# Dealing the MLP's hidden columns over the partitions in turn: longer runs for w2, a column step in w1's weights, alpha loaded in place

## The chip, the cores and the metric

The kernel runs on one core of one Trainium2 chip. A core has a matrix engine (TensorE, in the profile PE, with its weight loads listed apart as PEld), three engines that work on tiles (VectorE, DVE; ScalarE, ACT; GpSimd, POOL), a queue processor (SyncE, SP), and 16 DMA engines that move data between the chip's memory and the core's own memory of 128 partitions (SBUF). TensorE writes into a second memory, PSUM, here six free banks of 512 columns and a separate pair of banks called A_ps.

The metric is the device time of one execution, in microseconds; lower is better. A comparison of two kernels uses executions of both on the same chip.

## The reference

A linear attention with a decay per head, followed by an MLP. For each batch and head, with blocks of 64 positions:

```python
intra = (q k^T * Dmask) v            # Dmask[i, j] = lam ** (i - j) for i >= j, else 0
inter = (q * lam ** (pos + 1)) @ kv_state
out   = intra + inter
kv_state = lam ** 64 * kv_state + (k * lam ** (63 - pos))^T v
```

q, k and v are 4 batches x 8 heads x 768 positions x 64, float32. The result, as 3072 tokens x 512 columns (x), goes into

```python
h = x @ w_in                         # w_in 512 x 2048
s = sin(alpha * h)                   # one alpha per column of h
g = h + s * s / (alpha + 1e-9)
y = g @ w_out                        # w_out 2048 x 512, y 3072 x 512
```

A hidden column f belongs to column f of w_in, alpha[f], and row f of w_out. In which order the 2048 hidden columns are worked on does not change y.

## The kernel before, in words

**Tiling.** The tokens are worked on in 6 chunks of 512 (index c). The attention of a chunk consists of four quads (t), each for some heads and positions of some batches: scale q and k with powers of lam (tags qs, ks), cast v (vs), transpose (Tq, Tk on TensorE for the first eight quads, a DMA transpose DT for the rest), the score matmuls S into A_ps, the mask (tag mask, line 914 for the first eight quads, 1092 later), the output matmuls O and the state Z, and the copy of the result into xT (tags x; line 988 in the first eight quads), which is the MLP's input, already transposed. A_ps has one copy, so the scores of a quad wait for the mask of the quad before.

The hidden columns are cut into 16 groups of 128 (index m). For a chunk and a group, grp_A (lines 1205 to 1249) does h^T = w1^T x with four matmuls: the stationary operand is 128 columns of w1 (128 x 128), the moving one is xT (512 tokens wide, or 256 where a group is done in halves: three pairs of groups in each of the chunks 0 and 1). So a partition of the result holds a hidden column. ACT then takes the sine with alpha as a scale per partition (tag sin, line 1231), one of POOL, DVE and ACT squares it (sq), and DVE forms g with r = 1 / (alpha + 1e-9) as a factor per partition (tag g, line 1243) into gT. grp_B (line 1283) multiplies gT with the 16 tiles of w2 (128 hidden columns x 512) for 128 tokens at a time and accumulates in PSUM; ACT or DVE copies the result out and a DMA stores it.

**Weights and alpha.** w1 is 128 partitions x 4 x 2048 and w2 is 128 x 16 x 512, both bfloat16, converted by POOL's DMAs on the way from float32. w_block (line 678) issues nine of them: w1 in a first block of two halves (w0, w0b) and three of 512 columns (w1, w2, w3), and w2 in four blocks of 512 rows (tags w4 to w7). Group m stands in columns 128 m to 128 m + 127 of w1, and row 128 m + p of w_out goes to partition p of tile m, in runs of one row (2 KB). alpha_ops (line 759) loads alpha as 16 rows of 128, transposes it on TensorE with the small identity identf (POOL, line 753), copies it out on ACT (tag alpha, line 765), adds 1e-9 on POOL (line 767) and takes the reciprocal on DVE (line 769).

**What sets the order.** Every operation is recorded with its engine, what it reads and writes, and an assumed duration (rec, rec_pe). The list ORDER in TUNE, written out by tag, fixes the order on each engine's queue; an engine does its list strictly in turn, so that a waiting operation holds up those behind it. schedule (line 287) runs through these lists with the assumed durations. It picks the PSUM banks, and before 60 us of its own time it puts matmuls on zeros (fill, line 641) where it expects TensorE to idle; their number comes from its assumed times. emit (line 478) turns what each operation depends on into semaphore waits. Operations without a name get tags c0, c1, ... in the order in which they are recorded.

**Where alpha's steps stand.** On ACT the issue of alpha's load comes after cT2.1. On POOL aeps (c30) stands between the issues of the weight blocks w3 and w2, with w4 next. On DVE the reciprocal (c31) stands between ks3.1 and Z0.1, mask2 and x1, the last of which writes a part of xT for the first MLP matmuls (A0.4h0e on TensorE). On TensorE the transpose (alpha T) stands between S1 and I0.

Of the kernel before, what the change touches and what calls it, by code (L numbers as in the profile page):

```python
# [5 lines left out]
ALU = mybir.AluOpType  # L6
# [71 lines left out]
    ORDER={'ACT': ['lam', 'c0', 'quad k0.1', 'c11', 'c13', 'c14', 'cT2.1', 'alpha in', 'c17', 'vs1', 'cT1.0', 'Zi0.1',  # L78
# [468 lines left out]
def bass_lightning_attn__then__act_snake_kernel(  # L547
# [36 lines left out]
    with es:  # L584
# [43 lines left out]
        alpha_r = sb("alpha_r", [NM, 128], F32)  # L628
        identf = sb("identf", [NM, NM], F32)
# [47 lines left out]

        def w_block(j, after=(), soft=()):
            if j == 0:
                for y in range(2):  # L680
                    cs = slice(256 * y, 256 * y + 256)
                    rec("POOL", lambda e, cs=cs: e.dma_start(
                        w1[:, :, cs], moe_w_in[:, cs].rearrange("(c p) f -> p c f", p=128)), 0, 0.8,
                        writes=[f"w1.0.{y}"], slot=f"w1_0{y}", work=1.6, weight=42.0, after=after, soft=soft,
                        tag="w0b" if y else "w0")
            elif j < 4:
                cs = slice(512 * j, 512 * (j + 1))
                src = moe_w_in[:, cs].rearrange("(c p) f -> p c f", p=128)
                wblk[j] = rec("POOL", lambda e: e.dma_start(w1[:, :, cs], src), writes=[f"w1.{j}"],
                              slot=f"w1_{j}", work=3.0, weight=80.0, after=after, soft=soft, tag=f"w{j}")  # L690
            else:
                j2 = j - 4
                src = moe_w_out[512 * j2:512 * (j2 + 1), :].rearrange("(m p) d -> p m d", p=128)
                wblk[j] = rec("POOL", lambda e: e.dma_start(w2[:, 4 * j2:4 * (j2 + 1), :], src),
                              writes=[f"w2.{j2}"], slot=f"w2_{j2}", work=3.0, weight=80.0, after=after, soft=soft,
                              tag=f"w{j}")

        def consts():
# [52 lines left out]
            for i in range(RZ):  # L751
                rec("DVE", lambda e, i=i: e.memset(Zi[i][:, :, :], 0.0), 0.2, writes=[f"Zi.{i}.0", f"Zi.{i}.1"])
            rec("POOL", lambda e: e.affine_select(
                out=identf[:, :], in_=maskf[0:NM, 0:NM], pattern=[[-1, NM]], compare_op=ALU.not_equal, fill=1.0,
                base=0, channel_multiplier=1), 0.2, reads=["maskf"], writes=["identf"])
# [3 lines left out]
        def alpha_ops():  # L759
            rec("ACT", lambda e: e.dma_start(alpha_r[:, :], moe_alpha.rearrange("(m p) -> m p", p=128)),  # L760
                writes=["alpha_r"], slot="alpha", work=0.1, weight=9.0, desc=16, tag="alpha in")
            vb = P.bank()
            rec_pe(lambda e: e.transpose(m_ps[vb.i][:, 0:NM], alpha_r[:, :], identf[0:NM, 0:NM]), [(FULL, 0.1)],
                   ["alpha_r", "identf"], [vb.key], claim=vb, tag="alpha T")
            rec("ACT", lambda e: e.copy(alpha_sb[:, :], m_ps[vb.i][:, 0:NM]), 0.2, reads=[vb.key], writes=["alpha"],
                frees=[vb], tag="alpha")
            rec("POOL", lambda e: e.tensor_scalar_add(aeps_sb[:, :], alpha_sb[:, :], 1e-9), 0.26,
                reads=["alpha"], writes=["aeps"])
            rec("DVE", lambda e: e.reciprocal(r_sb[:, :], aeps_sb[:, :]), 0.25, reads=["aeps"], writes=["r"])
# [435 lines left out]
        def grp_A(c, m, sq="POOL", half=None, early=0):  # L1205
# [10 lines left out]
            def pe(e, kcs=range(NKC)):  # L1216
                for i, mm in enumerate(ms):
                    for kc in kcs:
                        last = e.matmul(m_ps[vb.i][:, N * i:N * i + N], w1[:, kc, 128 * mm:128 * (mm + 1)],  # L1219
                                        xT[x][:, kc, ts], start=(kc == 0 and i == 0), stop=(kc == NKC - 1),  # L1220
                                        skip_group_check=True)
                return last
# [7 lines left out]
            for i, mm in enumerate(ms):  # L1230
                rec("ACT", lambda e, i=i, mm=mm: e.activation(  # L1231
                    t16[tt][:, N * i:N * i + N], m_ps[vb.i][:, N * i:N * i + N], ACTF.Sin,
                    scale=alpha_sb[:, mm:mm + 1]), 0.26 + N / 1200, 0.145 + N / 1200,
                    reads=[vb.key, "alpha"], writes=[f"t.{tt}"], tag=f"sin{c}.{mm}" + ("" if half is None else f"h{half}"))
# [220 lines left out]
```

## Time and profile before

| | |
|---|---|
| median of 3 executions | 213.55 us (213.46 to 213.74) |
| span of the profiled execution, first to last instruction | 211.8 us |
| the profiled execution's own time beside its span | not recorded; the median is 1.75 us above the span |
| TensorE (PE) busy | 202.6 us, 2108 matmuls listed |
| weight loads (PEld) busy | 108.9 us |
| DVE, ACT, POOL busy | 128.5, 128.7, 120.7 us |
| DMA | 33.92 MB in 86491 packets |
| granted TensorE clock, mean | 0.998 |

How to read it. A row of an instruction list gives its start from the beginning of the span and its duration in us, the engine, the line in the kernel, what it writes and reads, and in brackets how long its engine was idle before it and what ended that idle time. Rows with "x4" stand for four instructions in a row. "SPq", "ACTq" and "POOLq" are the issues of DMAs. A row of a DMA queue has its packets, the MB moved, and the time its packets took as a share of all 16 DMA engines; shares of queues add up to more than 100% where packets overlap. q0 is POOL's queue (the weights), q1 SP's (q, k, v and the transposes), q10 ACT's (lam, one k load, alpha, the results). A row of a DMA issue has how many such DMAs there were, their size by the destination's elements, and the median time from the issue to the landing. In the chain that ended last each piece is followed back to what released it.

### The profile page before, as it was taken

Reading aid. Unit: us, or ns where it says so; the run is one execution under the profiler, and the core shown is the slowest. Engines: PE = TensorE matmul, PEld = TensorE weight load, DVE = VectorE, ACT = ScalarE, POOL = GpSimd, SP = SyncE. Lnnn points to the kernel's source line nnn. Section 1 sums busy time; section 2 is a strip of 40 time slices with the busy share of each in tenths; the row PEclk is TensorE's granted clock in tenths of the full one; section 3 lists DMA queues with packets and bytes.
Section 4 is the critical chain, followed back from the end, with each engine's and each line's share of the span. In section 5 each row is a group of like instructions: output and inputs, shape, how many; then the busy total and the mean of one; then the engine's idle time right before and its main releaser. Section 6 shows DMA issues by size and latency. Waiting matters only on the chain.

```text
span 211.8 us, 5201 instructions
## 1 busy us (share of the span) xinstructions
PE 202.6 (96%) x2108; PEld 108.9 (51%) x2139; DVE 128.5 (61%) x229; ACT 128.7 (61%) x246; POOL 120.7 (57%) x135
## 2 busy tenths in 40 slices
PE   7798999999999999999999999999999999999994
PEld 5455756555774555444554455454544544444454
DVE  4598899678889971285753475474556521456700
ACT  3146899835599755767648756757786434646231
POOL 3772174511537772899945899687397335144500
PEclk9999999999999999999999999999999999999999
DMA  6999999998999968899779999957033011101214
GB/s 182 314 238 235 208 251 237 216 223 169 244 182 197 190 117 190 200 199 197 189 154 209 198 183 240 177 137 171 3 99 148 4 50 50 53 0 50 101 54 149
DMA packets 86491, 33.92 MB, mean 160 GB/s; under 512 B 68274, under 2 KB 83522, under 8 KB 86466
## 3 DMA queue, kind: packets, MB, share of 16 engines
q1 hardware_dynamic: 77552, 22.88, 55.3%
q0 software_dynamic: 4752, 4.19, 12.1%
q10 hardware_dynamic: 4162, 6.50, 8.7%
q8 instruction: 17, 0.28, 0.6%
q14 instruction: 8, 0.07, 0.1%
HBM read 27.27 MB, written 6.29 MB: 158 GB/s over the span
## 4 chain that ended last, share of the span: by engine, by line
PE 85%; DVE 6%; DMA 2%; issue 2%; ACTq 1%; SPq 1%; ACT 1%; POOL 0%; POOLq 0%
PE M_ps L1219 39%; PE M_ps L1296 36%; DMA q<-in_q_dram 2%; PE M_ps L1120 2%; PE M_ps L1100 1%; DVE gT L1243 1%; PE A_ps L1080 1%; PE M_ps L866 1%; PE M_ps L971 1%; DVE S_m L1092 1%; DVE S_m L914 1%; PE M_ps L956 1%; PE M_ps L1264 1%; DVE q2o L825 1%; PE A_ps L909 1%
## 5 line engine op out<-in xcount | busy, mean ns | idle before, releaser
L1239 POOL TENSOR_TENSOR u<-t 128x512 bf16<-128x512 bf16 x69 | 70.6, 1041 | 55.0 <-ACT t L1231 51.7
L1243 DVE SCALAR_TENSOR_TENSOR gT<-u,r_sb,M_ps 128x512 bf16<-128x512 bf16 (+1 forms) x108 | 70.2, 684 | 45.1 <-POOL u L1239 43.8
L1219 PE MATMUL M_ps<-xT,w 128*128 128x512 bf16 (+1 forms) x425 | 88.1, 355 | 0.6 <-DVE gT L1243 0.2
L1296 PE MATMUL M_ps<-w,gT 128*128 128x512 bf16 x347 | 83.6, 379 | 2.5 <-issue 1.9
L1231 ACT ACTIVATE t<-M_ps,alpha_sb 128x512 bf16<-128x512 f32 (+1 forms) x108 | 65.7, 640 | 27.7 <-PE M_ps L1219 26.0
L1219 PEld LDWEIGHTS M_ps<-xT,w 128*128 128x128 bf16 x432 | 41.4, 98 | 40.1 <-DVE gT L1243 0.5
L1296 PEld LDWEIGHTS M_ps<-w,gT 128*128 128x128 bf16 x368 | 34.3, 98 | 39.2 <-DVE gT L1243 0.4
L1044 POOL TENSOR_TENSOR qk<-k,Lk 128x512 bf16<-128x512 f32 x16 | 16.6, 1044 | 9.9 <-DMA k<-in_k_dram 9.9
L1092 DVE TENSOR_TENSOR S_m<-A_ps,maskl 128x768 bf16<-128x768 f32 x16 | 15.3, 955 | 8.5 <-PE A_ps L1080 8.4
L1312 ACT COPY osb<-M_ps 128x512 f32<-128x512 f32 x20 | 11.7, 585 | 13.4 <-PE M_ps L1296 13.4
L1044 POOL TENSOR_TENSOR qk<-q,Lq 128x512 bf16<-128x512 f32 x16 | 16.6, 1041 | 2.2 <-DMA q<-in_q_dram 2.2
L1172 ACT CAST xT<-M_ps 128x512 bf16<-128x512 f32 x16 | 9.4, 586 | 13.3 <-PE A_ps L1080 11.4
L641 PE MATMUL M_ps<-zeros 128*128 128x512 bf16 (+1 forms) x45 | 10.7, 390 | 1.4 <-DVE zeros L702 1.2
L1195 ACT CAST Zq<-Zf 64x256 bf16<-64x256 f32 x24 | 9.6, 400 | 1.4 <-DVE Zf L1185 0.7
L914 DVE TENSOR_TENSOR S_m<-A_ps,maskq 128x1024 bf16<-128x1024 f32 x8 | 9.7, 1212 | 1.0 <-PE A_ps L909 0.5
L1239 DVE TENSOR_TENSOR u<-t 128x512 bf16<-128x512 bf16 x13 | 7.3, 560 | 4.4 <-ACT t L1231 4.4
L1055 ACT CAST v<-v 128x512 bf16<-128x512 f32 x16 | 9.7, 618 | 0.3 <-DMA v<-in_v_dram 0.2
L838 POOL TENSOR_TENSOR qk<-k,Lk 128x256 bf16<-128x256 f32 (+1 forms) x7 | 4.9, 703 | 8.6 <-DMA k<-in_k_dram 8.0
L1238 ACT ACTIVATE u<-t 128x512 bf16<-128x512 bf16 x14 | 8.7, 636 | 0.3
L869 ACT COPY qkT<-M_ps 128x512 bf16<-128x512 bf16 x5 | 2.9, 587 | 7.3 <-PE M_ps L866 7.3
L641 PEld LDWEIGHTS M_ps<-zeros 128*128 128x128 bf16 x48 | 4.6, 122 | 4.4 <-issue 1.7
L1189 DVE TENSOR_TENSOR Zf<-M_ps,Zf 128x256 f32<-128x256 f32 x10 | 4.2, 418 | 4.2 <-ACT xT L1172 4.2
(87 smaller groups left out, 139.8 us busy)
## 6 DMA issues: line engine op xcount, KB each, us to landing
out_dram<-osb ACTq DMA_DIRECT2D x23, 256.0 KB, 2.8
q<-in_q_dram SPq DMA_DIRECT2D x20, 256.0 KB, 4.8
k<-in_k_dram SPq DMA_DIRECT2D x34, 128.0 KB, 4.2
v<-in_v_dram SPq DMA_DIRECT2D x32, 128.0 KB, 4.0
v<-in_v_dram SPq DMA_DIRECT2D x8, 256.0 KB, 8.2
w<-in_moe_w_out_dram POOLq DMA_DIRECT2D x4, 512.0 KB, 11.5
k<-in_k_dram SPq DMA_DIRECT2D x6, 256.0 KB, 10.5
w<-in_moe_w_in_dram POOLq DMA_DIRECT2D x3, 512.0 KB, 11.0
```

Of the source, the lines that this page charges most:

```text
L641: last = e.matmul(m_ps[i][:, 0:c], zeros[:, 0:128], zeros[:, 0:c])
L914: rec("DVE", lambda e: e.tensor_tensor(S_m[jm][:, :, :].rearrange("p (h a b) c -> p h a (b c)", h=2, a=2), Av().rearrange("p h (a x) -> p ...
L1044: rec(en, lambda e, L=L, gs=slice(g0, g0 + m): e.tensor_tensor(o[:, :, gs], i[:, :, gs], L, ALU.mult), *(((0.65, 0.58) if en == "DVE" else ...
L1055: rec("ACT", lambda e: e.copy(o, i), 0.613, 0.51, reads=rd, writes=[f"v2.{c}"], tag=f"vs{t}")
L1092: rec("DVE", lambda e: e.tensor_tensor(S_m[jm][:, :, :].rearrange("p (a b) c -> p a (b c)", a=4)[:, :, 0:192], A_ps[:, :, :].rearrange("p ...
L1195: rec(en, lambda e, rows=rows, en=en: (e.copy if en == "ACT" else e.tensor_copy)(Zq[jj][rows, :, rows], Zf[jj][rows, :, :].rearrange("p i ...
L1219: last = e.matmul(m_ps[vb.i][:, N * i:N * i + N], w1[:, kc, 128 * mm:128 * (mm + 1)], xT[x][:, kc, ts], start=(kc == 0 and i == 0), stop=( ...
L1231: rec("ACT", lambda e, i=i, mm=mm: e.activation(t16[tt][:, N * i:N * i + N], m_ps[vb.i][:, N * i:N * i + N], ACTF.Sin, scale=alpha_sb[:, m ...
L1239: return e.tensor_tensor(u16[tt][:, :], t16[tt][:, :], t16[tt][:, :], ALU.mult)
L1243: rec("DVE", lambda e, i=i, mm=mm: e.scalar_tensor_tensor(out=gT[g][:, mm, ts], in0=u16[tt][:, N * i:N * i + N], scalar=r_sb[:, mm:mm + 1] ...
L1296: last = e.matmul(m_ps[vb.i], gT[g][:, m, 128 * s4:128 * (s4 + 1)], w2[:, m, :], start=(m == 0 or (split and m == 8)), stop=(m == NM - 1 o ...
L1312: rec("ACT", lambda e: e.copy(osb[o][:, :], m_ps[vb.i]), 0.585, 0.48, reads=[vb.key], writes=[f"o.{o}"], frees=[vb], tag=f"o{gsi}")
```

## The change

The hidden columns are given to the partitions in another order. In the first 512 columns two groups share 256 neighbouring columns: partition p takes columns 2 p and 2 p + 1, one for each group. In the other 1536, four groups share 512 columns, and partition p takes four neighbours.

- w2: the rows that a partition needs are neighbours in w_out now, so a load moves runs of 2 rows (4 KB) in the first block and 4 rows (8 KB) in the others, instead of single rows of 2 KB. Bytes and number of loads stay.
- w1 is loaded as before. grp_A takes the 128 columns of a group from it with a step of 2 or 4 columns (cols).
- alpha comes straight into its place, partition by group, with two DMAs of runs of 2 and of 4 floats on ACT's queue. The identity identf, the transpose on TensorE with its PSUM bank, and the copy on ACT go away. aeps waits for both DMAs, and so does the first sine.
- ORDER has the new tags in the old places; c28 (identf) and the alpha entries are gone, c30 and c31 are now called aeps and r, and ACT's c29 is c28.

```diff
@@ ORDER
-    ... 'cT2.1', 'alpha in', 'c17', 'vs1', 'cT1.0', 'Zi0.1', 'alpha', 'x0', ... 'Zi2.0', 'c29',
+    ... 'cT2.1', 'alpha in0', 'alpha in', 'c17', 'vs1', 'cT1.0', 'Zi0.1', 'x0', ... 'Zi2.0', 'c28',
-    (DVE) ... 'mask1', 'ks3.1', 'c31', 'Z0.1', 'mask2', 'x1',
+    (DVE) ... 'mask1', 'ks3.1', 'r', 'Z0.1', 'mask2', 'x1',
-    (PE) ... 'Z1', 'Z0', 'S1', 'alpha T', 'I0',
+    (PE) ... 'Z1', 'Z0', 'S1', 'I0',
-    (POOL) ... 'w0b', 'w0', 'c28', 'ks3.0', 'vs0', 'w3', 'c30', 'w2', 'w4',
+    (POOL) ... 'w0b', 'w0', 'ks3.0', 'vs0', 'w3', 'aeps', 'w2', 'w4',
@@ w_block
+        def cols(m):
+            n, f = (2, 256 * (m // 2)) if m < 4 else (4, 512 * (m // 4))
+            return slice(f + m % n, f + 128 * n, n)
...
-                src = moe_w_out[512 * j2:512 * (j2 + 1), :].rearrange("(m p) d -> p m d", p=128)
-                wblk[j] = rec("POOL", lambda e: e.dma_start(w2[:, 4 * j2:4 * (j2 + 1), :], src),
+                n = 4 if j2 else 2
+                src = moe_w_out[512 * j2:512 * (j2 + 1), :].rearrange("(a p m) d -> p a (m d)", p=128, m=n)
+                dst = w2[:, 4 * j2:4 * (j2 + 1), :].rearrange("p (a m) d -> p a (m d)", m=n)
+                wblk[j] = rec("POOL", lambda e: e.dma_start(dst, src),
@@ consts
-            rec("POOL", lambda e: e.affine_select(
-                out=identf[:, :], in_=maskf[0:NM, 0:NM], ...), 0.2, reads=["maskf"], writes=["identf"])
@@ alpha_ops
-            rec("ACT", lambda e: e.dma_start(alpha_r[:, :], moe_alpha.rearrange("(m p) -> m p", p=128)),
-                writes=["alpha_r"], slot="alpha", work=0.1, weight=9.0, desc=16, tag="alpha in")
-            vb = P.bank()
-            rec_pe(lambda e: e.transpose(m_ps[vb.i][:, 0:NM], alpha_r[:, :], identf[0:NM, 0:NM]), [(FULL, 0.1)],
-                   ["alpha_r", "identf"], [vb.key], claim=vb, tag="alpha T")
-            rec("ACT", lambda e: e.copy(alpha_sb[:, :], m_ps[vb.i][:, 0:NM]), 0.2, reads=[vb.key], writes=["alpha"],
-                frees=[vb], tag="alpha")
+            for y, (m0, n, na) in enumerate(((0, 2, 2), (4, 4, 3))):
+                rec("ACT", lambda e, m0=m0, n=n, na=na: e.dma_start(
+                    alpha_sb[:, m0:m0 + n * na].rearrange("p (a m) -> p a m", m=n),
+                    moe_alpha[128 * m0:128 * (m0 + n * na)].rearrange("(a p m) -> p a m", p=128, m=n)),
+                    writes=[f"alpha.{y}"], slot=f"alpha{y}", work=0.2, weight=9.0, desc=128 * na,
+                    tag="alpha in" + ("" if y else "0"))
+            al = ["alpha.0", "alpha.1"]
             rec("POOL", lambda e: e.tensor_scalar_add(aeps_sb[:, :], alpha_sb[:, :], 1e-9), 0.26,
-                reads=["alpha"], writes=["aeps"])
-            rec("DVE", lambda e: e.reciprocal(r_sb[:, :], aeps_sb[:, :]), 0.25, reads=["aeps"], writes=["r"])
+                reads=al, writes=["aeps"], tag="aeps")
+            rec("DVE", lambda e: e.reciprocal(r_sb[:, :], aeps_sb[:, :]), 0.25, reads=["aeps"], writes=["r"], tag="r")
@@ grp_A
-                        last = e.matmul(m_ps[vb.i][:, N * i:N * i + N], w1[:, kc, 128 * mm:128 * (mm + 1)],
+                        last = e.matmul(m_ps[vb.i][:, N * i:N * i + N], w1[:, kc, cols(mm)],
...
-                    reads=[vb.key, "alpha"], writes=[f"t.{tt}"], ...
+                    reads=[vb.key, "alpha.0", "alpha.1"], writes=[f"t.{tt}"], ...
```

More of the change, by code (lines that the diff above doesn't have):

```diff
@@ L77 @@
     FSL=0.05,
-    ORDER={'ACT': ['lam', 'c0', 'quad k0.1', 'c11', 'c13', 'c14', 'cT2.1', 'alpha in', 'c17', 'vs1', 'cT1.0', 'Zi0.1',
[1 row of a table removed]
+    ORDER={'ACT': ['lam', 'c0', 'quad k0.1', 'c11', 'c13', 'c14', 'cT2.1', 'alpha in0', 'alpha in', 'c17', 'vs1', 'cT1.0', 'Zi0.1',
[1 row of a table added]
                    'sin0.4h0', 'x3', 'sin0.2h0', 'sin0.5h0', 'sin0.7', 'sin0.3h0', 'sin0.1', 'sin0.4h1', 'sq0.1',
@@ L627, in bass_lightning_attn__then__act_snake_kernel @@
         Lk = sb("Lk", [128, NE, H], F32)
-        alpha_r = sb("alpha_r", [NM, 128], F32)
-        identf = sb("identf", [NM, NM], F32)
         alpha_sb = sb("alpha_sb", [128, NM], F32)
@@ L752, in consts @@
                 rec("DVE", lambda e, i=i: e.memset(Zi[i][:, :, :], 0.0), 0.2, writes=[f"Zi.{i}.0", f"Zi.{i}.1"])
-            rec("POOL", lambda e: e.affine_select(
-                out=identf[:, :], in_=maskf[0:NM, 0:NM], pattern=[[-1, NM]], compare_op=ALU.not_equal, fill=1.0,
-                base=0, channel_multiplier=1), 0.2, reads=["maskf"], writes=["identf"])
             rec("ACT", lambda e: e.activation(junk[:, :], maskf[:, 0:1], ACTF.Sin), 1.3,
@@ L1233, in grp_A @@
                     scale=alpha_sb[:, mm:mm + 1]), 0.26 + N / 1200, 0.145 + N / 1200,
-                    reads=[vb.key, "alpha"], writes=[f"t.{tt}"], tag=f"sin{c}.{mm}" + ("" if half is None else f"h{half}"))
+                    reads=[vb.key, "alpha.0", "alpha.1"], writes=[f"t.{tt}"], tag=f"sin{c}.{mm}" + ("" if half is None else f"h{half}"))
             def square(e):
```

10 rows, old and new, of the table ORDER are left out of this document.

## The prediction

> **What bounds the kernel now.** I read the page first: its busy shares, then the chain that ended last.
>
> ```profile
> span 211.8 us, 5201 instructions
> PE 202.6 (96%) x2108; PEld 108.9 (51%) x2139; DVE 128.5 (61%) x229; ACT 128.7 (61%) x246; POOL 120.7 (57%) x135
> PE 85%; DVE 6%; DMA 2%; issue 2%; ACTq 1%; SPq 1%; ACT 1%; POOL 0%; POOLq 0%
> ```
>
> TensorE looks full and carries 85% of the chain, but its busy time also counts matmuls on zeros, and a share is a mean over stages. So next the busy time by stage (columns: stretch, its length, then busy us and instructions of PE, PEld, DVE, ACT, POOL, the granted clock, the DMA share, GB/s).
>
> ```profile
> 24.00:60.00 36.00, 35.41 (x402) 21.47 (x406) 30.66 (x64) 26.30 (x57) 14.63 (x17) 1.00 1.11 220
> 60.00:110.00 50.00, 48.94 (x544) 24.98 (x552) 34.34 (x57) 36.11 (x68) 38.34 (x38) 1.00 0.93 184
> 110.00:160.00 50.00, 48.84 (x559) 25.07 (x566) 25.93 (x39) 33.27 (x60) 37.81 (x38) 1.00 0.82 157
> 160.00:205.50 45.50, 45.13 (x258) 21.10 (x261) 20.25 (x30) 21.27 (x35) 19.00 (x19) 1.00 0.13 47
> ```
>
> From 24 to 205.5 us TensorE idles 0.59 + 1.06 + 1.16 + 0.37 = 3.2 us of 181.5, at full clock. A transfer that ends sooner has almost nothing to win there. What can move the end is the start of that dense stretch, and the length of its matmuls. So I followed the chain, and the instructions around it, before 24 us.
>
> ```profile
> 16.53 0.97 PE M_ps L641 x4
> 18.58 0.70 DVE xT L988
> ```
> ```profile
> 9.11 0.34 ACTq L760 DMA_DIRECT2D alpha_r<-in_moe_alpha_dram  x1
> 11.84 0.39 POOL L753 TENSOR_SCALAR_AFFINE_SELECT identf<-maskf 16x16 f32<-16x16 f32 x1
> 14.91 0.17 ACT L765 COPY alpha_sb<-M_ps 128x16 f32<-128x16 f32 x1 [0.56 <-PE M_ps L763]
> 15.18 0.26 POOL L767 TENSOR_SCALAR aeps_sb<-alpha_sb 128x16 f32<-128x16 f32 x1 [0.92 <-ACT alpha_sb L765]
> 15.50 0.81 POOL L689 DMA_DIRECT2D w<-in_moe_w_in_dram  x1
> 15.97 0.42 DVE L838 TENSOR_TENSOR qk<-k,Lk 128x256 bf16<-128x256 f32 x1
> 16.30 0.25 DVE L769 RECIPROCAL r_sb<-aeps_sb 128x16 f32<-128x16 f32 x1
> 16.32 0.75 POOL L694 DMA_DIRECT2D w<-in_moe_w_out_dram  x1
> 16.47 0.23 DVE L999 COPY Zf<-M_ps 128x128 f32<-128x128 f32 x1
> 16.61 1.21 DVE L914 TENSOR_TENSOR S_m<-A_ps,maskq 128x1024 bf16<-128x1024 f32 x1
> 18.58 0.69 DVE L988 CAST xT<-M_ps 128x512 bf16<-128x512 f32 x1 [0.76 <-PE M_ps L926]
> 25.67 1.04 POOL L1239 TENSOR_TENSOR u<-t 128x512 bf16<-128x512 bf16 x1 [8.60 <-ACT t L1231]
> ```
>
> The instruction to watch is the reciprocal of alpha (L769, tag r). It sits in DVE's fixed order, with no idle time around it, in front of Zf, the mask of quad 2 and the write of xT (L988) that the first MLP matmuls read. The only slack behind it is the 0.76 us that DVE waits before L988.
>
> **The change, part by part.**
>
> *Alpha's removed steps.* Out go POOL's identf (0.39 us), a TensorE transpose of 16 rows, and ACT's copy (0.17 us, after 0.56 idle). TensorE fills the same stretch with zeros, ACT and POOL are waiting there, and DVE, which sets the pace, loses nothing: 0. The second alpha transfer costs ACT one more issue of 0.34 us; if ACT were not waiting there it would cost that, and it is the cost without cover. POOL's aeps and DVE's r stay, in place.
>
> *Alpha's transfer.* Before: 16 runs of 512 B, one per DMA engine. After: runs of 8 B (2 floats, 256 of them) and of 16 B (4 floats, 384): 640 runs, so 40 per engine plus 2 semaphore writes, 42 packets. They share the engines with the weights (queue q0) and with the loads of q, k, v (q1). Rows, in this order: the transfer of alpha; q10, alpha's queue, in 13.0 to 13.5; q0 and q1 in 13 to 14; q1 in 14 to 15, 15 to 16 and 16 to 17.
>
> ```profile
> alpha_r<-in_moe_alpha_dram ACTq DMA_DIRECT2D x1, 8.0 KB, 4.9
> ...
> q10 hardware_dynamic: 29, 0.01, 6.9%
> ...
> q0 software_dynamic: 135, 0.14, 81.0%
> q1 hardware_dynamic: 139, 0.07, 34.8%
> ...
> q1 hardware_dynamic: 289, 0.15, 59.3%
> ...
> q1 hardware_dynamic: 189, 0.15, 58.5%
> ...
> q1 hardware_dynamic: 164, 0.16, 59.1%
> ```
>
> In 13 to 14 the two queues move 135 and 139 packets although one's are far larger: the engines take one packet from each queue in turn. So a queue that always has a packet gets about 139 / 16 = 8.7 turns per us on an engine, then 18, 11.8 and 10.3 in the next three. Alpha's packets ran from about 13.1 (29 of its 32 lie before 13.5) and it landed at 9.11 + 4.9 = 14.0. From 13.1, 42 turns are 7.8 + 18 + 11.8 = 37.6 by 16.0, and 4.4 / 10.3 = 0.4 more: 16.4, and 0.4 from last packet to landing as before: 16.8. Its own turns, and a second transfer that starts after the first, add some tenths: I take 17.2. Ends: 14.0 (as now, if small runs share a turn) and 19.6 (all 42 at 8.7 per us, and the second transfer 1.3 us later).
>
> [...]
>
> *What waits for it.* aeps on POOL starts 0.1 us after alpha, takes 0.26, r starts 0.1 later; from r's start to the mask's start is 0.31 and the mask takes 1.21. So the mask ends at landing + 1.98, and L988 slips once that passes 18.58: a landing after 16.6. At 17.2 the slip is **0.6 us**. Behind the waiting r stand Zf, the mask, L988, then the Zq copies that quads 1 and 2 wait for; the dense stretch begins that much later, and with 3.2 us of idle spread thin over it I give nothing back. POOL waits at aeps too, and behind it L689 and L694 issue the next two weight blocks 2 us later: hidden, because those blocks queue behind an earlier one that lands at 13.45 + 11.0 = 24.5 (the weights' row of that issue is quoted below), and POOL's next work starts at 25.67. Without that cover it would be 2 us.
>
> *The w2 loads.* First the weight block issued at 13.45; then q0 in 19 to 20 (1 KB read per packet), q0 and q1 in 36 to 37 (2 KB read), q1 alone in 9 to 10, the k load issued at 27.22, and the POOL work on k.
>
> ```profile
> w<-in_moe_w_in_dram POOLq DMA_DIRECT2D x1, 512.0 KB, 11.0
> ...
> q0 software_dynamic: 212, 0.11, 78.2%
> ...
> q0 software_dynamic: 145, 0.14, 84.6%
> q1 hardware_dynamic: 145, 0.07, 36.3%
> ...
> q1 hardware_dynamic: 587, 0.29, 120.3%
> ...
> k<-in_k_dram SPq DMA_DIRECT2D x1, 256.0 KB, 11.5
> ```
> ```profile
> 39.68 0.80 POOL L838 TENSOR_TENSOR qk<-k,Lk 128x256 bf16<-128x256 f32 x1
> 45.49 0.62 POOL L838 TENSOR_TENSOR qk<-k,Lk 128x256 bf16<-128x256 f32 x1 [5.02 <-DMA k<-in_k_dram]
> ```
>
> A packet costs 0.782 x 16000 / 212 = 59 ns for 1 KB and 0.846 x 16000 / 145 = 93 ns for 2 KB, so about 25 + 34 per KB: 161 ns at 4 KB, 297 at 8 KB. Before: 2048 x 93 = 191 engine-us; after: 256 x 161 + 384 x 297 = 155. That frees 36 / 16 = 2.2 us of all engines. But turns go one for one, so beside 8 KB packets q1 gets fewer: a pair now takes 16 / 145 = 110 ns where 93 + 40 were counted (0.83), then 0.83 x 337 = 280 ns. Three blocks take 3 x 128 / 57 per us = 6.7 us instead of 10.6, in which q1 moves 384 packets instead of 971; at 587 per us alone it has caught up by 8.7. At worst a k load is 4.0 us late: the one landing at 27.22 + 11.5 = 38.7 comes by 42.7. POOL then waits at 39.68, with 5.02 idle before 45.49 to take it; the load that ends this idle comes earlier. I take 0 for the end; the ends are the 2.2 us gained, of which TensorE's idle could use perhaps 1, and 3 lost if TensorE waits for one of those loads.
>
> *The weights with a column step.* 336 matmuls of 512 columns and 96 of 256 now load weights 2 or 4 elements apart. No load in this trace steps. The rows: all loads of L1219, the nearest slower one (f32, 128 columns), the 256-column matmuls, and a run of 512-column ones.
>
> ```profile
> L1219 PEld LDWEIGHTS M_ps<-xT,w 128*128 128x128 bf16 x432 | 41.4, 98 | 40.1 <-DVE gT L1243 0.5 <-ACT xT L1172 0.4 <-issue 0.3
> ```
> ```profile
> 3.10 0.28 PEld L722 LDWEIGHTS A_ps<-lnlam,ones 1*128 1x128 f32 x1 [0.20 <-issue]
> 19.73 0.83 PE L1219 MATMUL M_ps<-xT,w 128*128 128x256 bf16 x6
> ```
> ```profile
> 159.16 3.45 PE M_ps L1219 x16
> ```
>
> The matmuls follow each other every 3.45 / 16 = 0.216 us at 512 columns and about 0.11 at 256 (0.83 for six). A load that stays near 98 ns is hidden under either: 0. At the f32 load's 280 ns it would cost 336 x 0.064 + 96 x 0.17 = 38 us. I take 0, since tile and type are those of the first row.
>
> [...]
>
> **Sum.** 0.6 us on the span. What lies around the span, 213.55 - 211.8 = 1.75 us, I leave as it is; no time of the profiled execution beside its span is given, so the sum stands on the median: **214.1 us**, slower by 0.3%. About 0.2% (0.43 us) is what a measurement can tell.
>
> **The rivals.**
> 1. *Alpha still lands before 16.6* (runs of one transfer share a turn, or the start is earlier). Then nothing on the path moves: 213.5. Against it: one-for-one counts.
> 2. *Faster.* The four zero matmuls in the chain at 16.53 (0.97 us) end just before the work that releases L988, and DVE idles 0.76 there, mask already done. The planner sets their number from its own times, from which the transpose, its bank and the copy now vanish; if it puts in one or none, and alpha lands before 15.9, L988 starts when the mask ends: up to 0.74 less, 212.8. For it: chain and idle agree; against it: the work beside them is unchanged.
> 3. *Stepped loads are slow.* From 110 ns on they show under 256 columns, from 216 under all. At twice 98: 96 x 0.086 = 8 us, 222; at the f32 price 251.
> 4. *w2's large packets starve q1*, and TensorE, whose order is fixed, waits for k: 2 to 3 us, 216.3. It decides once a k or v load for quads 5 to 7 is later than DVE and POOL can hide.
>
> **How the numbers follow.** Forecast 0.46 (its own range 213.6 to 216.5, by landings to 19.6), rivals 0.18, 0.20, 0.10, 0.06. The range 212.8 to 217.0 takes in all but rival 3 and the far ends of 2 and 4, about 0.17. Slower by over 0.2%: 0.41 of the forecast, rivals 3 and 4, 0.57; within: 0.05 and rival 1, 0.23; faster: 0.20.
>
> **What would show it.** Alpha's second transfer landing at 17 rather than 14, aeps near 17.3, r near 17.7 with an idle wait before it, L988 near 19.2, and the same spacing from there on. Weight loads of L1219 at 98 ns and the 0.216 and 0.11 us spacing would show that the step is free; w2's packets fewer (640 for 2048) and its last block landing some us sooner with TensorE no denser, that the long runs are hidden. Wrong it would be made by an alpha at 14, by loads above 110 ns, or by a wait of TensorE for k between 35 and 55 us.

## The result: 216.26 us after 213.65, and where the time went

The changed kernel took 216.26 us (median of 4 executions, 215.46 to 216.59), the kernel before 213.65 beside it (4 executions): 1.0113 times as long, 95% interval 1.0089 to 1.0136. The profiled execution took 216.31 us, 1.8 us of it outside its span.

The page of the changed kernel: the span, the busy shares and the chain that ended last.

```profile
span 214.5 us, 5193 instructions
PE 203.5 (95%) x2105; PEld 113.9 (53%) x2136; DVE 128.0 (60%) x229; ACT 128.5 (60%) x245; POOL 119.4 (56%) x134
PE 86%; DMA 7%; DVE 2%; issue 2%; ACTq 1%; SPq 1%; ACT 1%; POOL 0%; POOLq 0%
```

The busy shares say almost nothing. The chain does: DMA has gone from 2% to 7% of it. The chain's pieces in order of time name the transfer, and the instruction list before 23 us shows who waits for it.

```profile
9.15 9.63 DMA alpha_sb<-in_moe_alpha_dram
```
```profile
18.94 0.26 POOL L768 TENSOR_SCALAR aeps_sb<-alpha_sb 128x16 f32<-128x16 f32 x1 [5.10 <-DMA alpha_sb<-in_moe_alpha_dram]
19.24 0.25 DVE L770 RECIPROCAL r_sb<-aeps_sb 128x16 f32<-128x16 f32 x1 [3.27 <-POOL aeps_sb L768]
20.00 1.91 PE L639 MATMUL M_ps<-zeros 128*128 128x512 bf16 x4 [2.73 <-DVE Zf L1000]
20.68 0.68 DVE L989 CAST xT<-M_ps 128x512 bf16<-128x512 f32 x1
22.62 1.12 PE L1220 MATMUL M_ps<-xT,w 128*128 128x256 bf16 x6
```

Alpha's second transfer, issued at 9.15, lands at 18.78 us. POOL waits 5.10 us for it, DVE 3.27 us at r, and TensorE 2.73 us for the Zf that stands behind r. The write of xT (L989, L988 before) starts at 20.68, which was 18.58. Two sines, one at the start and one near the end (before, then after), show that nothing else happened later.

```profile
23.82 0.47 ACT L1231 ACTIVATE t<-M_ps,alpha_sb 128x256 bf16<-128x256 f32 x1 [0.39 <-PE M_ps L1219]
193.50 0.69 ACT L1231 ACTIVATE t<-M_ps,alpha_sb 128x512 bf16<-128x512 f32 x1 [0.24 <-PE M_ps L1219]
```
```profile
26.46 0.47 ACT L1232 ACTIVATE t<-M_ps,alpha_sb 128x256 bf16<-128x256 f32 x1 [0.39 <-PE M_ps L1220]
196.22 0.69 ACT L1232 ACTIVATE t<-M_ps,alpha_sb 128x512 bf16<-128x512 f32 x1 [0.23 <-PE M_ps L1220]
```

The lag is 26.46 - 23.82 = 2.64 us at the second sine and 196.22 - 193.50 = 2.72 at this late one. The whole loss is there by 26 us, and 170 us of dense work carry it unchanged to the end. But xT was only 20.68 - 18.58 = 2.10 us late. The other half microsecond appears between 20 and 24 us, where the busy times by stage show the granted clock (the column behind POOL's).

```profile
20.00:21.00 1.00, 1.00 (x3) 0.44 (x3) 1.00 (x2) 0.98 (x3) 0.87 (x2) 0.50 1.25 220
21.00:22.00 1.00, 1.00 (x11) 0.16 (x12) 0.89 (x4) 0.25 (x1) 0.00 (x0) 0.50 1.22 215
22.00:23.00 1.00, 1.00 (x26) 0.74 (x25) 0.70 (x3) 0.80 (x4) 0.00 (x0) 0.50 1.24 208
23.00:24.00 1.00, 1.00 (x13) 0.90 (x11) 0.99 (x1) 1.00 (x1) 0.00 (x0) 0.88 1.24 204
```

After its wait TensorE runs at half clock. With 0.91 in the stretch from 19 to 20 us and 0.88 from 23 to 24 it lasts 0.18 + 3 + 0.24 = 3.4 us. The six 256-column matmuls at 22.62 take 1.12 us instead of 0.83.

Why alpha is late shows in the queues, packets by window of 1 us: 13 to 14 and 14 to 15 of the changed kernel, then 14 to 15 of the kernel before.

```profile
q0 software_dynamic: 136, 0.14, 81.6%
q1 hardware_dynamic: 134, 0.07, 33.5%
q10 hardware_dynamic: 133, 0.00, 7.5%
...
q0 software_dynamic: 156, 0.12, 72.9%
q1 hardware_dynamic: 163, 0.08, 39.5%
q10 hardware_dynamic: 158, 0.00, 8.9%
```
```profile
q0 software_dynamic: 128, 0.10, 59.8%
q1 hardware_dynamic: 289, 0.15, 59.3%
```

136, 134 and 133: the three queues get the same number of packets, although the share of the engines' time is 81.6% for one and 7.5% for the other. A packet of alpha is one run of 8 or 16 bytes (with two more on each engine, 672 in all, as the prediction counted). In the profiled execution of the kernel before, the weights' queue had a lull from 14 to 15 us, and q1 got 289 packets; in the changed kernel's all three queues stayed full, and there were 163. The lull was that execution's, not the kernel's: POOL's weight issues stood some 0.4 us later in it (7.59 us for the first, 7.18 in the changed kernel), ahead of everything that the change touches on POOL. In the other 13 traces of this case the first weight issue stands at 7.09 to 7.28 us, so the lags above are taken against a start that was some 0.4 us late.

The other two parts of the change, in the groups of loads, the queues' totals, and the queues at 38 to 39 us of the changed kernel:

```profile
L1220 PEld LDWEIGHTS M_ps<-xT,w 128*128 128x128 bf16 x432 | 46.2, 109 | 36.1 <-ACT xT L1173 0.4 <-DVE gT L1244 0.4 <-issue 0.3
```
```profile
q0 software_dynamic: 3344, 4.19, 11.1%
...
w<-in_moe_w_out_dram POOLq DMA_DIRECT2D x4, 512.0 KB, 8.7
...
q0 software_dynamic: 48, 0.19, 92.8%
q1 hardware_dynamic: 54, 0.03, 14.5%
```

The loads of w1 take 109 ns on the mean (98 before; the mean mixes two steps, see the run with a step of 8), under matmuls that follow each other every 216 ns where they are 512 columns wide. w2's packets of 8 KB take 0.928 x 16000 / 48 = 309 ns each, and its loads land in 8.7 us (11.5 before).

### The profile page after: what moved, and what is told of

It reads as the page before. It is cut to its first block, busy times and chain, and to the rows that moved or that the text cites. A ratio compares the mean times of both kernels' runs of the same rounds, so it can differ in the third digit from the quotient of the medians.

```text
span 214.5 us, 5193 instructions
## 1 busy us (share of the span) xinstructions
PE 203.5 (95%) x2105; PEld 113.9 (53%) x2136; DVE 128.0 (60%) x229; ACT 128.5 (60%) x245; POOL 119.4 (56%) x134
## 4 chain that ended last, share of the span: by engine, by line
PE 86%; DMA 7%; DVE 2%; issue 2%; ACTq 1%; SPq 1%; ACT 1%; POOL 0%; POOLq 0%
PE M_ps L1220 39%; PE M_ps L1297 36%; DMA alpha_sb<-in_moe_alpha_dram 4%; PE M_ps L1121 2%; DMA q<-in_q_dram 2%; PE M_ps L1101 1%; PE A_ps L1081 1%; PE M_ps L867 1%; PE M_ps L972 1%; PE M_ps L639 1%; PE M_ps L1265 1%; PE M_ps L957 1%; PE A_ps L910 1%; ACTq L1276 1%; PE M_ps L1132 1%
## 5 line engine op out<-in xcount | busy, mean ns | idle before, releaser
L1220 PEld LDWEIGHTS M_ps<-xT,w 128*128 128x128 bf16 x432 | 46.2, 109 | 36.1 <-ACT xT L1173 0.4
L1093 DVE TENSOR_TENSOR S_m<-A_ps,maskl 128x768 bf16<-128x768 f32 x16 | 15.3, 955 | 8.6 <-PE A_ps L1081 8.4
L1045 POOL TENSOR_TENSOR qk<-q,Lq 128x512 bf16<-128x512 f32 x16 | 16.6, 1040 | 0.0
```

The source lines that it names most:

```text
L1045: rec(en, lambda e, L=L, gs=slice(g0, g0 + m): e.tensor_tensor(o[:, :, gs], i[:, :, gs], L, ALU.mult), *(((0.65, 0.58) if en == "DVE" else ...
L1093: rec("DVE", lambda e: e.tensor_tensor(S_m[jm][:, :, :].rearrange("p (a b) c -> p a (b c)", a=4)[:, :, 0:192], A_ps[:, :, :].rearrange("p ...
L1220: last = e.matmul(m_ps[vb.i][:, N * i:N * i + N], w1[:, kc, cols(mm)], xT[x][:, kc, ts], start=(kc == 0 and i == 0), stop=(kc == NKC - 1), ...
```

## The experiments

Theory after the result: alpha's 640 short runs are the whole loss, by a DVE wait of 2.1 us at the xT write and a half clock of about 0.5 us. Rivals: the long w2 runs or the stepped loads have a share; the half clock lies beside the wait and costs nothing; the short runs are slow by themselves, whoever shares the engines. Each ratio is against executions of the kernel before on the same chip.

**One part at a time.** Alpha's part alone, with w1 and w2 as before:

```diff
-                src = ...rearrange("(a p m) d -> p a (m d)", p=128, m=n)
+                src = ...rearrange("(m p) d -> p m d", p=128)
...
-    w1[:, kc, cols(mm)]
+    w1[:, kc, 128 * mm:128 * (mm + 1)]
```

> Only alpha's part of the change: two DMAs of 8 B and 16 B runs, no identity, no transpose; w1's columns and w2's rows as before. (Alpha is dealt and the columns are not, so each column gets another column's alpha; the instructions are the same.) Theory A, alpha lands late and holds DVE's reciprocal: alpha lands at 18.8 us as in the changed kernel, DVE waits 3 us before the reciprocal, and the time is 2.6 us above before, ratio 1.010 to 1.014. Theory B, the weights' part costs the time: ratio 0.998 to 1.002.

216.99 us, ratio 1.0148 (1.0125 to 1.0170). The instruction list has the same wait. A half clock of 3.4 us is there too, but later, from 21.2 to 24.6 us: the zero matmuls behind the wait still ran at full clock.

```profile
18.91 0.26 POOL L766 TENSOR_SCALAR aeps_sb<-alpha_sb 128x16 f32<-128x16 f32 x1 [4.99 <-DMA alpha_sb<-in_moe_alpha_dram]
19.21 0.25 DVE L768 RECIPROCAL r_sb<-aeps_sb 128x16 f32<-128x16 f32 x1 [3.16 <-POOL aeps_sb L766]
```

The weights' part alone, with alpha's one transfer, transpose and copy as before:

```diff
-                src = ...rearrange("(m p) d -> p m d", p=128)
+                src = ...rearrange("(a p m) d -> p a (m d)", p=128, m=n)
...
-    w1[:, kc, 128 * mm:128 * (mm + 1)]
+    w1[:, kc, cols(mm)]
```

> Only the weights' part: w2 in runs of 4 and 8 KB, w1's weights with a column step; alpha by 16 runs, identity, transpose and copy as before, in the old order. (The columns are dealt and alpha is not, so each column gets another column's alpha.) Theory A: alpha lands at 14, no wait, ratio 0.998 to 1.002; the loads of w1 at 109 ns instead of 98 stay hidden. Theory B: ratio 1.008 or more, through loads or through late k.

213.25 us, ratio 0.998 (0.9951 to 1.0009). So alpha's part is the loss, and the weights' part costs nothing. The 0.4 us between the medians is no gain of the long runs in this trace: its first weight issue comes at 7.13 us (7.59 in the trace of the kernel before), its second sine at 23.35 (23.82), and the late sine at 193.08 (193.50). The lead is there before w2 is loaded. Whether the kernel before starts late in every execution, its one trace can't say.

**r out of the way.** The changed kernel with aeps behind two weight issues on POOL, and r behind Z1.1 on DVE:

```diff
-    (POOL) ... 'w3', 'aeps', 'w2', 'w4',
+    (POOL) ... 'w3', 'w2', 'w4', 'aeps',
-    (DVE) ... 'ks3.1', 'r', 'Z0.1', 'mask2', 'x1', ... 'Z1.1', 'x2',
+    (DVE) ... 'ks3.1', 'Z0.1', 'mask2', 'x1', ... 'Z1.1', 'r', 'x2',
```

> The whole change, with two entries of the order moved: aeps behind the issues of the next two weight blocks on POOL, and the reciprocal behind Z1.1 on DVE, where DVE waited 0.35 us for TensorE. Alpha still lands near 18.8. Theory A, the loss is that the reciprocal stands in front of the mask: no wait of DVE at 16, no half clock, first MLP matmul at 19.0 to 19.8, and a time at or below before: 212.7 to 213.8, ratio 0.995 to 1.001. Rival, late alpha costs by itself, or the step and the long runs do: ratio 1.005 or more.

214.87 us, ratio 1.0065 (1.0042 to 1.0088). DVE's wait and the half clock were gone and the first MLP matmul came at 18.61 us, 1.1 us earlier than in the kernel before. And yet the kernel was slower than the one before: the second sine led by 1.32 us, the late one lagged by 0.14. At 42 us TensorE waits for something else.

```profile
41.49 0.69 DVE L826 TENSOR_TENSOR q2o<-q,Lq 128x512 bf16<-128x512 f32 x1 [2.86 <-DMA q<-in_q_dram]
42.33 0.38 PE L867 MATMUL M_ps<-ident,q2o 128*128 128x128 bf16 x4 [0.77 <-DVE q2o L826]
```

Was it the earlier weight issues, or the 8 KB runs? One run moves only r on DVE (POOL keeps its order, so the weight blocks start at 19.3 and 20.1 us), another keeps both moves and loads w2 in 2 KB runs:

```diff
b1: -    (DVE) ... 'ks3.1', 'r', 'Z0.1',        + ... 'Z1.1', 'r', 'x2',
b2: the two moves above, and
-                src = ...rearrange("(a p m) d -> p a (m d)", p=128, m=n)
+                src = ...rearrange("(m p) d -> p m d", p=128)
```

> The changed kernel with one edit: the reciprocal r of alpha stands later in DVE's order (behind the second Z copy, ahead of the third x copy); POOL's order is left as it is, so aeps still waits for alpha at about 18.9 us and the two weight blocks behind it still start at 19.4 and 20.2 us (in the run with both moved, r late on DVE and aeps late on POOL, they started at 13.8 and 14.5 us, and q of the seventh block came late: TensorE waited 0.77 us before L867 at 42.33 us). Theory A (the early weight blocks are what held up q): first MLP matmul at 18.6 us, no wait at 42 us, time 212.4 to 213.2, against 213.7 before. Theory B (the 8 KB reads of w2 hold up q whenever they come): the wait at 41 to 43 us stays, and the time is near 214.9.

> The kernel with r late on DVE and aeps late on POOL (214.87 us, TensorE waits 0.77 us for q at 42.33 us), with one more edit: w2 is loaded in the 2 KB runs of the kernel before (its rows then do not belong to w1's stepped columns, so the products of the second MLP matmul are those of other rows; sizes and order of the work are the same). Theory A (early weight blocks): the wait for q stays, 214.5 to 215.2. Theory B (8 KB reads): q lands in time, no wait at 42 us, 213.0 or less.

214.22 us, ratio 1.0035 (1.0018 to 1.0052), and 214.22, ratio 1.0028 (1.0010 to 1.0046). First the run with r alone moved: the scores and what follows them on TensorE, the first MLP matmul, the wait; then the one with 2 KB runs.

```profile
15.60 0.42 PE L910 MATMUL A_ps<-qTo,qkT 64*64 64x128 bf16 x16 [0.17 <-DVE S_m L915]
16.07 0.31 PE L927 MATMUL M_ps<-v,qk 64*64 64x64 bf16 x8
18.57 0.84 PE L1220 MATMUL M_ps<-xT,w 128*128 128x256 bf16 x6
42.30 0.38 PE L867 MATMUL M_ps<-ident,q2o 128*128 128x128 bf16 x4 [0.52 <-DVE q2o L826]
```
```profile
37.50 1.25 PE L1295 MATMUL M_ps<-w,gT 128*128 128x512 bf16 x5 [0.57 <-DMA w<-in_moe_w_out_dram]
```

Neither expectation held. With late weight blocks the wait for q stays, so the early blocks weren't its cause. With 2 KB runs q comes in time, but w2 itself is waited for. The two transfers of q of 512 KB took 15.3 us from issue to landing with long runs in both kernels, 13.0 with 2 KB runs, 10.8 in the kernel before. Here the run length decided which load was late. That one is late at all fits the earlier start, but these runs also carry alpha's 640 runs, and no run separates the two. In the run with r alone moved the lead of 1.20 us at 37.4 us (38.60 before) had become a lag of 0.07 at 58.85 (58.78 before). The waits don't make up the whole time: the run with 2 KB runs still led by 0.29 us at the late sine (193.21). In the three runs with r moved, in the order in which they stand here, the last block of narrow matmuls starts at 205.59, 205.56 and 205.17 us (205.32 before), and the span ends 7.2, 6.7 and 7.2 us after it (6.5 before). So 0.2 to 0.7 us more go at the last stores; why, no run shows.

**Zero matmuls taken away.** The changed kernel without the fill from 18 us of the planner's time:

```diff
-        P = Program(NPS, fill=zero_mms, fill_until=60.0, ...
+        P = Program(NPS, fill=zero_mms, fill_until=18.0, ...
```

> The whole change, but the planner puts in no zero matmuls from 18 us of its time on, so that the five that stand between O1 and Z2 go. They are issued only when the late reciprocal lets Zf free a bank, and then run at half clock for 1.9 us in front of Z2. Theory C, the zero matmuls add to the loss: first MLP matmul 0.6 to 1.0 us earlier (near 21.8), time 215.3 to 215.8, ratio to before 1.008 to 1.010. Rival, they fill time in which TensorE would wait for xT anyway, or TensorE idles longer and stays at half clock longer: no gain, 216.0 or more.

218.09 us, ratio 1.0207 (1.0187 to 1.0226): the theory that they add to the loss missed, and the rival held. Alpha landed as before, the idle time of TensorE grew to 3.57 us, and the half clock lasted 6.8 us instead of 3.4 (0.52 from 20 to 21 us, 0.56 from 26 to 27).

```profile
20.91 0.31 PE L927 MATMUL M_ps<-v,qk 64*64 64x64 bf16 x4 [3.57 <-ACT v L853]
```
```profile
20.00:26.00 6.00, 5.09 (x90) 4.18 (x92) 4.21 (x10) 3.75 (x9) 0.77 (x2) 0.50 1.24 211
```

The second sine came at 27.60 us, 1.14 later than in the changed kernel. So with the matmuls on zeros, which looked like a burden, the idle time and the half clock were shorter (2.73 and 3.4 us). (This execution, the longest of the five at 219.25 us, lost another 1.2 us near 90 us, where POOL waited for a k load.)

**Alpha issued first.** The two transfers moved in ACT's order from behind cT2.1 to behind the first k load:

```diff
-    (ACT) 'lam', 'c0', 'quad k0.1', 'c11', 'c13', 'c14', 'cT2.1', 'alpha in0', 'alpha in', 'c17',
+    (ACT) 'lam', 'c0', 'quad k0.1', 'alpha in0', 'alpha in', 'c11', 'c13', 'c14', 'cT2.1', 'c17',
```

> The changed kernel with one edit: ACT issues the two alpha transfers ahead of its other early work, at about 2 to 4 us in place of 8.7 and 9.2, before the first weight block's queue is busy. Theory (alpha is late because its 42 packets per engine take turns with two other queues from 11.6 us on): alpha lands before 14 us, aeps and r do not wait, no half clock at 20 to 23 us; time 213.2 to 214.0. Rival (the short runs cost the engines their own time wherever they stand, some 42 packets of 60 ns or more on each engine): the first q, k and v loads land 1 to 3 us later, the first matmuls too, and the time is 214.5 to 217.

214.10 us, ratio 1.0005 (0.9989 to 1.0021). Both theories had a part. The wait for alpha is gone, and the same 640 runs land 6.5 us after their issue, not 9.6:

```profile
14.99 0.26 POOL L768 TENSOR_SCALAR aeps_sb<-alpha_sb 128x16 f32<-128x16 f32 x1
16.96 0.24 DVE L770 RECIPROCAL r_sb<-aeps_sb 128x16 f32<-128x16 f32 x1
```
```profile
alpha_sb<-in_moe_alpha_dram ACTq DMA_DIRECT2D x1, 6.0 KB, 6.5
```

But the first loads of q and k paid for it: TensorE's transposes that start at 8.26 us in the changed kernel start at 9.27 here, and the first MLP matmul comes at 20.79 (19.73 before). One row of the order takes back nearly the whole loss.

**The clock alone.** Eight zero matmuls in TensorE's wait, added to the S result that lies in PSUM (this changes values, not the amount of work):

```diff
+                    rec_pe(warm, [(FULL, 8 * 0.2157)], ["S0", "S1", "zeros"], wr, tag="warm")
-    (PE) ... 'O1', 'Z2', 'S3',
+    (PE) ... 'O1', 'warm', 'Z2', 'S3',
```

> The changed kernel with eight zero matmuls of 512 columns added behind the second output matmuls of the start (O1), where TensorE waits 2.73 us for alpha's r and Zf: they add zero to the S result that lies in PSUM anyway, so they need no bank of their own and end before DVE reads it. The wait for alpha stays (aeps at 18.9 us, r at 19.2). Theory (of the 2.6 us that the change lost, part is TensorE's half clock at 20 to 23 us, which its idle time brings about): granted clock 1.00 throughout, dense stretch 0.5 to 0.9 us earlier than in the changed kernel, time 215.3 to 215.8 (ratio 1.008 to 1.010). Rival (the half clock lies beside the wait and costs nothing of its own): 216.2.

216.72 us, ratio 1.0153 (1.0116 to 1.0190). It doesn't answer its question. In the profiled execution alpha landed at about 17, so the eight matmuls themselves held up the mask.

```profile
17.18 0.26 POOL L768 TENSOR_SCALAR aeps_sb<-alpha_sb 128x16 f32<-128x16 f32 x1 [2.57 <-DMA alpha_sb<-in_moe_alpha_dram]
20.01 1.22 DVE L922 TENSOR_TENSOR S_m<-A_ps,maskq 128x1024 bf16<-128x1024 f32 x1 [2.14 <-PE A_ps L917]
```

It answered another one by chance: in this execution the weights' queue was nearly empty from 14 to 15 us (8 packets).

```profile
q1 hardware_dynamic: 501, 0.28, 92.6%
q10 hardware_dynamic: 449, 0.01, 25.4%
q0 software_dynamic: 8, 0.01, 4.3%
```

449 packets of alpha in that 1 us, 158 in the changed kernel. There the short runs weren't slow by themselves; the 158 went beside 156 packets of the weights, which read 1 or 2 KB each, the 449 beside 8. This is one execution with a lull that nobody set up.

To empty that queue on purpose, I issued the fourth w1 block behind aeps:

```diff
-    (POOL) ... 'vs0', 'w3', 'aeps', 'w2', 'w4',
+    (POOL) ... 'vs0', 'aeps', 'w3', 'w2', 'w4',
```

> The changed kernel with one edit on POOL: the fourth column block of w1 (issued at 13.03 us, ahead of aeps) is issued behind aeps. Theory (alpha is late because the weights' queue always has a packet ready, so that each engine gives alpha's queue one short run for every 2 KB of weights): the weights' queue runs dry between about 13.5 us and aeps, alpha's packets go by at two to four times the rate (the run with zero matmuls in the wait, in which that queue happened to be empty at 14 to 15 us, showed 449 alpha packets in that 1 us against 158 in the changed kernel), alpha lands at 15.5 to 17 us, DVE's r starts before 17.3 us, no half clock; time 213.0 to 214.3, unless the later weight block is waited for at 26 to 29 us, which would show there. Rival (the short runs have a rate of their own, about 150 per us): alpha lands near 18.8 us as before, and the time stays at 216.3.

216.66 us, ratio 1.0115 (1.0094 to 1.0137). The queue didn't run dry: the blocks issued before kept it full (13 to 14 us below), and alpha landed as late as ever. So the edit didn't make the condition that the theory needs, and its time decides nothing on the turns.

```profile
q0 software_dynamic: 134, 0.14, 80.4%
q1 hardware_dynamic: 134, 0.07, 33.5%
q10 hardware_dynamic: 134, 0.00, 7.5%
```
```profile
19.10 0.25 DVE L770 RECIPROCAL r_sb<-aeps_sb 128x16 f32<-128x16 f32 x1 [3.16 <-POOL aeps_sb L768]
19.78 1.03 PE L639 MATMUL M_ps<-zeros 128*128 128x512 bf16 x4 [2.53 <-DVE Zf L1000]
21.37 0.83 PE L1220 MATMUL M_ps<-xT,w 128*128 128x256 bf16 x6
25.85 0.47 ACT L1232 ACTIVATE t<-M_ps,alpha_sb 128x256 bf16<-128x256 f32 x1 [0.39 <-PE M_ps L1220]
```

But it priced the clock. Here r starts 0.14 us sooner than in the changed kernel, TensorE idled 2.53 us, and the clock stayed at 1.00: four zero matmuls take 1.03 us, not 1.91. The second sine comes at 25.85 instead of 26.46. Of these 0.61 us 0.14 are r's, so the half clock cost about 0.5 us. (The run with alpha's part alone, with r at 19.21 and the second sine at 26.62, gives 0.77 - 0.11, about 0.7.) (Its time shows none of it: at 88 us POOL waited for a k load, and the lag of the sines behind the kernel before went from 2.0 to 3.6 us.)

**Alpha in long rows.** The weights as in the changed kernel; alpha in five whole rows (2 of 1 KB, 3 of 2 KB), six small transposes that take every second or fourth column, two ACT copies; the order of the kernel before:

```diff
+                    alpha_r[y][:, :], moe_alpha[f:f + (2 + y) * w].rearrange("(a p) -> a p", p=w)),
...
+                        last = e.transpose(m_ps[vb.i][:, m0 + na * m:m0 + na * (m + 1)], alpha_r[y][:, m::n],
+                                           identf[0:na, 0:na])
```

> The weights as in the changed kernel, and alpha as whole rows as in the kernel before: two transfers (2 runs of 1 KB, 3 runs of 2 KB; five runs in place of 640) and six small transposes with a column step in place of one, then two ACT copies, in the order of the kernel before. If the 640 short runs are the whole loss: alpha lands before 16 us, no stall of DVE, time as of the run with the weights' part alone, 213.25, at most 0.3 above it for the five added transposes and the second copy (ratio 0.998 to 1.000). If the weights' part needs the alpha part's other timing to be harmless, above 214.

213.32 us, ratio 0.9981 (0.9964 to 0.9997), as expected. aeps started at 16.22 us without a wait for alpha. With r moved back on DVE as well:

```diff
-    (DVE) ... 'mask1', 'ks3.1', 'c31', 'Z0.1',
+    (DVE) ... 'mask1', 'ks3.1', 'Z0.1', ... 'Z1.1', 'c31', 'x2',
```

> The kernel with the weights' part and alpha in five long rows (213.32 us, first MLP matmul at 19.42 us), with r late on DVE too. In the three runs with r late the first MLP matmul came at 18.6 to 18.8 us and the lead of 1.2 us was gone by 42 to 58 us, where TensorE waited for q, or with 2 KB runs for w2. Theory A (the loads of the first 45 us bound that stretch, however alpha comes): the lead at the start grows by 0.7 us, is lost again at 38 to 56 us, and the time is 213.2 to 214.3. Theory B (alpha's 640 packets are what makes q late there): the lead stays, and the time is near 212.6.

213.16 us, ratio 0.9973 (0.9961 to 0.9985), the lowest median, though its interval overlaps those of the weights' part alone and of the run without the move. Neither theory was tested: the first MLP matmul came at 19.41, as without the move, so there was no lead to lose. r, no longer late, isn't what sets the start; TensorE's queue is. Here the scores come at 16.00 us, behind alpha's transposes, and three zero matmuls follow them (16.35), so that the write of xT starts at 18.26. With alpha's steps gone and r moved the scores came at 15.60, no zero matmul followed (rows above), and that write started at 17.22.

**A step of 8.** From the kernel with the weights' part alone, the columns of m = 8 to 15 at step 8:

```diff
-            n, f = (2, 256 * (m // 2)) if m < 4 else (4, 512 * (m // 4))
+            n, f = (2, 256 * (m // 2)) if m < 4 else (4, 512) if m < 8 else (8, 1024)
```

> The kernel with the weights' part alone (213.25 us; weight loads of the first MLP matmul 109 ns with steps of 2 and 4, 98 ns without a step before), with the columns of m = 8 to 15 taken at step 8 over two weight blocks (they then belong to other rows of w2 and other alphas; sizes and order of the work are the same, but the first use of these columns waits for both blocks). Theory A (a stepped load costs the same at any step): mean 109 ns as at 2 and 4. Theory B (the cost grows with the bytes that a row spans): half the loads at 150 to 220 ns, mean 130 to 165. In both cases the loads lie beside matmuls of 273 ns and more: time 213.2 to 213.8.

213.69 us, ratio 0.9994 (0.9981 to 1.0006). The loads of that line take 123 ns on the mean, but the mean mixes the steps. Three groups of chunk 4 show them apart: m = 2 at step 2, m = 6 at step 4, m = 10 at step 8 (shortest, median and longest load in ns).

```profile
L1225 PEld LDWEIGHTS M_ps<-xT,w x4: 98/98/98, 155.6 to 156.2; 128*128 128x128 bf16 x4
L1225 PEld LDWEIGHTS M_ps<-xT,w x4: 112/113/113, 157.3 to 158.0; 128*128 128x128 bf16 x4
L1225 PEld LDWEIGHTS M_ps<-xT,w x4: 143/143/144, 159.9 to 160.6; 128*128 128x128 bf16 x4
```

A step of 2 costs nothing, a step of 4 costs 15 ns, a step of 8 costs 45. The changed kernel has the same 98 ns in its group m = 2 and 113 to 114 in m = 6; its 109 is a mean of the two. The cost grows with the step, as theory B had it, but stays just under B's 150 ns. The loads stay hidden.

## Why the prediction was right in sign and short in size

The direction was right, and 216.26 us lies in its range; the forecast of 214.1 was 2.2 us short. By its steps, in the prediction's order:

- *What bounds the kernel.* Right for this kernel. The dense stretch carried the lag of 2.64 us to the end as it was, so only the start counted. It does not carry a lead in the same way: the kernels that started over 1 us earlier lost it by 58 us.
- *Alpha's removed steps, 0.* Right for the end. At the start they were worth something: with r out of the way the first MLP matmul came 1.16 us earlier, of which some 0.5 are the late start of the profiled execution before (7.59 for 7.09 us). By 58 us it was lost to late loads, which the prediction had not priced for an earlier start.
- *Alpha's transfer, landing at 17.2.* This is the step that failed: 18.78 us was measured. The counting, one packet from each queue in turn, was right to within a few packets (136, 134 and 133 from 13 to 14 us). The turns per us were read off the kernel before: 8.7, 18, 11.8, 10.3. Measured were (133, 158 and then by the same view 195 and 149 packets, over 16 engines) 8.3, 9.9, 12.2 and 9.3. The 18 came from the lull of the weights' queue in that one execution. The run with alpha in long rows, whose POOL work is that of the kernel before, has 179 weight and 182 q1 packets in the same 1 us: no lull. At the measured turns an average engine has done its 42 at about 17.2 us (an estimate from these rates), 0.8 later than the 16.4 of the prediction. With the 0.4 us to the landing that makes 17.6. The other 1.2 us are the stragglers: by 17 us all but 35 of 672 packets had gone, but the last five went at 18.0 to 18.5, and the landing came after them, where the prediction counted an average engine and took 0.4 us for all else. The upper end of 19.6 took this in.
- *What waits for it.* Right, order and threshold: 18.78 - 16.6 = 2.2 us of slip, 2.10 measured at L989.
- *The missing term.* TensorE's idle time behind r was not priced beyond the wait. After it stood 3.4 us of half clock, about 0.5 us. 2.1 + 0.5 makes the 2.6 of the medians.
- *w2's runs, 0.* Right: 0.998 alone. The priced packet of 297 ns measured 309. (By the prediction's own rates q1 has caught up at 8.0 us, from 384 + 587 (t - 6.7) = 145 t, not at 8.7; its 4.0 us do not depend on that.)
- *The step, 0.* Right for the time. The loads at step 4 took 113 ns, past the mark of 110 from which the prediction saw them show under 256 columns; but six such matmuls at step 4 took 0.83 us at full clock (21.37 us in the run with the fourth w1 block later), as before. Step 2 cost nothing (98 ns); step 4 cost 15 ns.
- *The rivals.* Alpha before 16.6: no, it landed at 18.78; with 136, 134 and 133 packets in 1 us alpha's queue got no more than one run for each packet of the others, so that small runs share a turn was not shown. Fewer zero matmuls: its first condition came true. None of the four stands behind the scores of the changed kernel (scores at 15.69 us, the next matmuls at 16.16), but late alpha hid it; with r moved it showed (18.57 us for 19.73), and loads ate it. w2's packets against q: not in the changed kernel, and that this rival's 216.3 us is the measured time is chance; but q was the next wait in both kernels that kept the long runs and started over 1 us earlier.

## What to carry over

When a transfer is cut into short runs, count its packets, not its bytes: here each waited its turn among what else the engines carried (133 short runs beside 136 and 134 packets in 1 us), and the count must be made to the last packet, with the queues full: a lull in the one execution that was profiled may not come again. Before pricing an earlier start, ask which load is late next (here a lead of 1.20 us at 37.4 us was gone by 58.85). Before reading a mean over loads or matmuls, look whether it mixes forms. A small operand that an in-order engine waits for was better loaded here in a few long rows and turned on chip (0.9981 of the kernel before), or issued before the bulk (1.0005), than in 640 short runs behind it (1.0113).

## What was not expected of the hardware

- Idle times of TensorE of 2.3 to 3.6 us had ends that their length doesn't sort: after 2.73 us the clock was 0.50 for 3.4 us, after 2.53 us in another kernel it stayed at 1.00, after 2.31 us in a third it fell to 0.50 some 1.5 us later, for 3.4 us, after 3.57 us it was 0.50 for 6.8 us. What decides between these ends, no run shows.
- It also differs between executions of one kernel. The mean clocks of the changed kernel's four were 0.992, 0.992, 1.000 and 0.990, and the one at 1.000 was the shortest (215.46 us; the others 216.22 to 216.59). The run with the fourth w1 block later, whose profiled execution kept its clock, had 0.992 in three of five, and there the time does not follow the clock (216.17 and 217.12 us at 1.000).
- The cost of the half clock was far less than half of its 3.4 us: 0.5 to 0.7 us. That 1.91 us of TensorE's work there, in the changed kernel, were matmuls on zeros is probably why; no run separates it.
- Queues that always had a packet got equal numbers of them, within a few, down to runs of 8 bytes beside 2 KB (136, 134 and 133 in 1 us).
- A weight load of 128 x 128 bf16 took 98 ns at a column step of 1 and of 2, 113 at 4, 143 at 8.
